# A decode-step gradient kernel on one core: 13 neighbouring rows of the MLP's inner index per partition

## The chip, the core and the metric

The kernel runs on one core of a Trainium2 chip. The metric is the device time of one execution in microseconds (us). A core has a matrix engine (PE, with its weight loads listed apart as PEld), a vector engine (DVE), a scalar engine (ACT), GpSimd (POOL), a sync engine (SP), and 16 DMA engines. DMAs are issued here by SP (queue q1, nearly all loads), POOL (queue q0, the big stores) and ACT (queue q10, the weight gradients' stores). SBUF has 128 partitions.

## The reference, cut to what matters

One transformer layer for a single new position per batch (two batches): layer norm, attention over a cache of 4096 keys and values with 32 heads of 128, then layer norm and an MLP of inner width 1728 with ReLU. The kernel computes the output and, for a given `grad_out`, the gradients of `x`, both caches, and all four weights.

```python
def _A_ref(x, k_cache, v_cache, wq, wo):           # x: 2 x 1 x 640, caches: 2 x 32 x 4096 x 128
    q = (x @ wq) per head
    p = softmax(q . k * 128 ** -0.5); o = p . v
    return o @ wo
def _B_ref(x, w1, w2):                             # w1: 640 x 1728, w2: 1728 x 640
    h = maximum(x @ w1, 0)
    return h @ w2
h = x + _A_ref(_layernorm(x), ...)
h2 = h + _B_ref(_layernorm(h), w1, w2)
# outputs: h2, and the vjp of (x, k_cache, v_cache, wq, wo, w1, w2) at grad_out
```

The caches and their gradients are 67 MB each for keys and for values, read and written once (values are read again for the backward pass, but for the 11 heads kept); they make up nearly all bytes. The MLP's inner index of 1728 is what the change is about: 13 x 128 = 1664 rows and a remainder of 64.

## The kernel before, in words

**Order of the work.** The program's order is written out by hand. A plan of iterations loops over the 64 pairs of batch and head. Phase 1 (`p1_iter`, one iteration per pair) loads K and V (1 MB each), transposes them on PE (L423, evicted by ACT at L428 or DVE at L426), multiplies with q (L436), takes the exponent (L512), forms `pk` on DVE (L464) and `m` and `u` on PE (L457, L486). After batch 0's 32 heads come seven iterations in which phase 1 goes on with batch 1 while batch 0's MLP is worked in between; from then on phase 2 (`p2_iter`) runs beside phase 1, and alone once phase 1 has ended. Phase 2 loads V again (`Wt`) for all but 11 kept heads, and forms the caches' gradients gK and gV on DVE (L818), which POOL stores 1 MB at a time (L856, L875).

**Background work.** Three lists of generators are advanced between the steps of the iterations. A `yield` of a number is the credit that a step takes; `turn()` hands out slots for long DVE products. `middle_gen(b)` is batch b's MLP: it finishes the attention output, normalises (`ln_fwd`), and computes the hidden layer `hf_ps` with w1 as the stationary operand, 14 chunks of up to 128 columns by 5 chunks of the input (L744, 70 matmuls). ReLU gives `acol` (L747). The gradient `ghfc` of the hidden layer (L763) is spread over all partitions as a row, `fbc`: `bcast_cols` makes four chunks at a time on PE (L622) in bank "bc" and ACT evicts them (L625). DVE then takes 15 products of w1 with a third of `fbc` each (L644, "junk" and "gx2p"). The evictions of `fbc` are interleaved: two before the first five products, one before the next five, one before the last. In batch 0 "bc" has two PSUM banks, in batch 1 one.

**w2.** `load_w2` brings w2 in three tiles, of six, six and two chunks. The first time (phase 1, after iterations 8, 13 and 18, for `ga_gen`) chunk c holds rows c*128 to c*128+127, one row of 1,280 bytes per partition and chunk. The second time (`mlp_out`, L698, in phase 2) the tile has whole stretches: partition p holds rows 13p to 13p+12, of which a tile takes six (7,680 bytes). To match, batch 1's middle computes the hidden layer once more in that order, for both batches: `ar_ps`, 65 matmuls whose weights are columns of w1 in steps of 13 (L755), into `arow` (L758).

**Stores of the weights' gradients.** `fin_gen` makes rows of the needed columns (`rows_of`: a copy `wide` at L888, a matmul at L893, an eviction at L895), and `outer_rows` their outer products: a matmul (L922) and an ACT eviction (L928) per 512 columns, several rows per partition gathered in a tile `ot`, and one store (L930, ACT's queue). w2's gradient `out_7` is stored from 96 partitions with 18 rows each, six rows at a time: three stores of 96 x 7,680 bytes.

**Queues.** SP issues all loads in the order of a list; its first two DMAs load A_x and grad_out into `xr` (L210, L211), ahead of wq (L378). SP waits when a tile's buffer is not free (12 big buffers, more in phase 2). ACT and PE execute in the program's order.

Of the kernel before, what the change touches and what calls it, by code (L numbers as in the profile page):

```python
# [7 lines left out]
FP32 = mybir.dt.float32  # L8
BF16 = mybir.dt.bfloat16
ALU = mybir.AluOpType  # L10
# [5 lines left out]
def kernel(  # L16
# [20 lines left out]
    nc = tc.nc  # L37
# [19 lines left out]

    def f_kc(c):
        return 128 if c < NFF else F_rem


    ctx.enter_context(tc.manual_schedule())
# [127 lines left out]
    arow = cols.tile([128, NF, B], BF16)  # L190
    OFc = cols.tile([128, H, B], BF16)
    GQc = cols.tile([128, H, B], BF16)
    qsc = cols.tile([128, H, B], BF16)
# [13 lines left out]
    nc.vector.memset(acol[:], 0.0)  # L207
    nc.vector.memset(ghfc[:], 0.0)

    nc.sync.dma_start(out=xr[0:2 * ND, :], in_=A_x.rearrange("b s (c p) -> (b s c) p", p=128))  # L210
    nc.sync.dma_start(out=xr[2 * ND:4 * ND, :], in_=grad_out.rearrange("b s (c p) -> (b s c) p", p=128))  # L211


    def colsum(src, n):
# [138 lines left out]
    FP = 6  # L353
    NW2 = -(-NF // FP)
    w2_tiles = {}

    def load_w2(k, tag, order="(c p) d -> p c d"):

        c0, c1 = k * FP, min(NF, (k + 1) * FP)
        t = take(tag, [128, FP, D], "w2_t")  # L360
        full = min(c1, NFF)
        if full > c0:
            nc.sync.dma_start(out=t[:, 0:full - c0, :],
                              in_=B_w2[0:NFF * 128, :].rearrange(order, p=128)[:, c0:full, :])
# [247 lines left out]
        nc.vector.tensor_tensor(out=Uc[:, b, :], in0=t[:], in1=rt[:, b, :], op=ALU.mult)  # L612


    def bcast_cols(colsrc, n, kc_of, dst):

        for c0 in range(0, n, 4):
            t = pst([128, 512], FP32, "bc", "bc_ps")
            w = 0
            for c in range(c0, min(n, c0 + 4)):  # L620
                kc = kc_of(c)
                nc.tensor.matmul(t[:, w:w + kc], lhsT=colsrc[0:kc, c:c + 1].to_broadcast([kc, 128]),  # L622
                                 rhs=ident_bf[0:kc, 0:kc], start=True, stop=True)
                w += kc
            nc.scalar.copy(out=dst[:, c0 * 128:c0 * 128 + w], in_=t[:, 0:w])  # L625
            yield

    def spread_cols(t, colsrc, n):
# [26 lines left out]
    def one(src, b):  # L655
        return src[:, :, b]
# [34 lines left out]
    def mlp_out():  # L691

        ml32 = small.tile([128, ND, B], FP32, tag="ml32", bufs=1, name="ml32")
        nc.vector.memset(ml32[:], 0.0)
        for k in range(NW2):
            while free["q"] < 1:
                yield
            t = load_w2(k, "q", "(p c) d -> p c d")  # L698
# [12 lines left out]
        nc.vector.tensor_copy(out=ml_bf[:], in_=ml32[:])  # L711
        y_bf = small.tile([128, B, ND], BF16, tag="y_bf", bufs=1, name="y_bf")
        nc.vector.tensor_tensor(out=y_bf[:].rearrange("p b c -> p c b"), in0=h1c[:], in1=ml_bf[:], op=ALU.add)
        yield from wait(3)
        for b in range(B):
            store_row(y_bf[:, b, :], ND, out_0[b].rearrange("s (c p) -> (s c) p", p=128))
            yield

    def middle_gen(b):
# [21 lines left out]
        for cf in range(NF):  # L741
            kc = f_kc(cf)
            for c in range(ND):
                nc.tensor.matmul(hf_ps[0:kc, cf:cf + 1], lhsT=w1_t[:, c, cf * 128:cf * 128 + kc],  # L744
                                 rhs=x2c[:, c, b:b + 1], start=(c == 0), stop=(c == ND - 1))
            yield 0.25
        nc.vector.tensor_scalar(out=acol[:, 0:NFF, b], in0=hf_ps[:, 0:NFF], scalar1=0.0, scalar2=None, op0=ALU.max)  # L747
        if F_rem:
            nc.vector.tensor_scalar(out=acol[0:F_rem, NFF, b:b + 1], in0=hf_ps[0:F_rem, NFF:NF],
                                    scalar1=0.0, scalar2=None, op0=ALU.max)  # L750
        if b == B - 1:
            ar_ps = pst([128, NFF, B], FP32, "mid", "ar_ps")
            for cf in range(NFF):
                for c in range(ND):
                    nc.tensor.matmul(ar_ps[:, cf, :], lhsT=w1_t[:, c, bass.ds(cf, 128, step=NFF)],  # L755
                                     rhs=x2c[:, c, :], start=(c == 0), stop=(c == ND - 1))
                yield 0.25
            nc.vector.tensor_scalar(out=arow[:, 0:NFF, :], in0=ar_ps[:], scalar1=0.0, scalar2=None, op0=ALU.max)  # L758
            if F_rem:
                nc.vector.tensor_copy(out=arow[:, NFF, :], in_=acol[:, NFF, :])  # L760
# [5 lines left out]
        gx2 = small.tile([128, 1, ND], FP32, tag="gx2", bufs=1, name="gx2")  # L766
        gx2p = small.tile([128, ND, 3], FP32, tag="gx2p", bufs=1, name="gx2p")
        FW = Dff // 3
        spread_f = bcast_cols(one(ghfc, b), NF, f_kc, fbc)
        have = 0  # L770
        for k in range(3):
            while have < min(Dff, (k + 1) * FW):
                next(spread_f)
                have += 512
                yield
            for c in range(ND):
                yield from turn()
                ttr(w1_t[:, c, k * FW:(k + 1) * FW], fbc[:, k * FW:(k + 1) * FW], gx2p[:, c, k:k + 1], FW)
                yield 0.85
# [99 lines left out]

    fw = [0]  # L880

    def rows_of(pool, col, n, name, tag):

        r = pool.tile([128, n * 128], BF16, tag=tag, bufs=2 if tag == "rD" else 1, name=name)
        for c0 in range(0, n, 4):
            cn = min(4, n - c0)
            w = FIN["wide"][(c0 // 4) % 2]
            nc.scalar.copy(out=w[:, 0:cn, :, 0:B], in_=col[:, c0:c0 + cn, None, :].to_broadcast([128, cn, 4, B]))  # L888
            yield
            yield  # L890
            t = pst([128, 512], FP32, "mid", "rw_ps")
            for k in range(cn):
                nc.tensor.matmul(t[:, k * 128:(k + 1) * 128], lhsT=w[:, k, :, :].rearrange("p q x -> p (q x)"),  # L893
                                 rhs=ident_bf[:], start=True, stop=True)
            nc.scalar.copy(out=r[:, c0 * 128:(c0 + cn) * 128], in_=t[:, 0:cn * 128])  # L895
            yield 0.7
        FIN[name] = r

    FIN = {}

    late = [False]

    def outer_rows(L, nrow, R, N, out_ap, cc):


        P = nrow // cc
        grp = max(1, min(cc, 4096 // N))
        out_v = out_ap.rearrange("(p c) n -> p c n", c=cc)
        for c0 in range(0, cc, grp):
            gn = min(grp, cc - c0)  # L910
            while not rested("f", 13):
                yield 0.0
            ot = take("f", [128, grp, N], "ot")
            todo = [(k, n0, min(512, N - n0)) for k in range(gn) for n0 in range(0, N, 512)]
            made = []
            for x in range(len(todo) + 1):
                if x < len(todo):
                    k, n0, nn = todo[x]
                    q = 32 * (fw[0] % 4)
                    o_ps = pst([128, 512], FP32, "o", "o_ps")  # L920
                    fw[0] += 1
                    nc.tensor.matmul(o_ps[0:P, 0:nn], lhsT=L[q:q + B, bass.ds(c0 + k, P, step=cc)],  # L922
                                     rhs=R[q:q + B, n0:n0 + nn], start=True, stop=True)
                    made.append((o_ps, k, n0, nn))
                    yield 0.3
                if x > 0:
                    o_ps, k, n0, nn = made[x - 1]
                    nc.scalar.copy(out=ot[0:P, k, n0:n0 + nn], in_=o_ps[0:P, 0:nn])  # L928
                    yield 0.3
            nc.scalar.dma_start(out=out_v[:, c0:c0 + gn, :], in_=ot[0:P, 0:gn, :])  # L930
            give(ot)

    def fin_gen(fin):
        FIN["wide"] = [fin.tile([128, 4, 4, 32], BF16, tag="wide", bufs=2, name="wide") for _ in range(2)]
# [299 lines left out]
```

## Time and profile before, and how to read it

| | |
|---|---|
| runs | 908.7, 908.89, 909.97 us; median 908.89 us |
| profiled execution | span 905.5 us from the first to the last instruction; it has no time of its own beside this span |
| busy | PE 742.8 us (82%), PEld 620.3, DVE 696.1 (77%), ACT 444.7, POOL 192.4 |
| bytes | 362.87 MB in 56,254 packets, mean 401 GB/s |
| DMA queues | q1 58.1% of the 16 engines' span, q0 35.9%, q10 4.2% |
| TensorE clock granted | 0.780 in the mean: full up to 293 us, mostly half after 470 us |
| w2's loads | four of 960 KB (two in each pass), and the remainders of 160 and 80 KB |
| out_7's stores | three of 720 KB |

The page shows the span in 40 equal slices of 22.6 us, each digit being the busy tenths of an engine. The DMA row is the mean busy share of the 16 DMA engines, and the row below what they moved. The chain of waits follows the last instruction back to what released it. In timelines a row has the start, the time, the engine, the line, the operation, and in brackets how long the engine sat idle and what ended it. Matmuls overlap with the loads of the next weights, so for the cost of a series of small matmuls the time of the series is divided by their number.

### The profile page before, as it was taken

The page shows a single profiled execution, that of the slowest core. Times are in us where ns is not written, and L with a number is a line of the kernel's source. Part 1 is how long each engine was busy: PE and PEld are TensorE (multiplying, and loading weights), DVE is VectorE, ACT ScalarE, POOL GpSimd, SP SyncE. Part 2 cuts the span into 40 slices and gives each one's busy share as a digit, 9 for nine tenths or more (in the row PEclk, how much of TensorE's full clock was granted, in tenths as well). Part 3 has the DMA queues.
Part 4 walks back from the last instruction along what each step waited for, and adds up shares of the span by engine and source line. Part 5 has one row for each costly group of instructions (what it writes and reads, how often), then busy time and mean ns, then how long its engine had stood idle before and what let it go on. Part 6 is the DMA issues. An engine that isn't in the chain of part 4 may idle for free.

```text
span 905.5 us, 24516 instructions
## 1 busy us (share of the span) xinstructions
PE 742.8 (82%) x10205; PEld 620.3 (68%) x10205; DVE 696.1 (77%) x1286; ACT 444.7 (49%) x1096; POOL 192.4 (21%) x330
## 2 busy tenths in 40 slices
PE   3999899899998997987968854877899879859880
PEld 3887788788887887876857744655667656645560
DVE  2666787777888796777869698986898349989982
ACT  1444343344554564554543434644576656637750
POOL 1344433443211110010011111211122111111120
PEclk9999999999999899999885776655555555555655
DMA  8999999999879999999999999999999999999997
GB/s 361 420 409 403 409 398 410 420 417 388 335 306 377 377 406 425 421 424 421 411 398 392 411 423 394 423 398 396 407 401 388 426 420 423 419 423 416 419 421 296
DMA packets 56254, 362.87 MB, mean 401 GB/s; under 512 B 5680, under 2 KB 11696, under 8 KB 15312
## 3 DMA queue, kind: packets, MB, share of 16 engines
q1 hardware_dynamic: 34704, 212.18, 58.1%
q0 software_dynamic: 18432, 134.23, 35.9%
q10 hardware_dynamic: 3008, 14.91, 4.2%
q8 instruction: 80, 1.31, 0.6%
q14 instruction: 30, 0.25, 0.1%
HBM read 212.16 MB, written 149.13 MB: 399 GB/s over the span
## 4 chain that ended last, share of the span: by engine, by line
PE 42%; DMA 25%; DVE 18%; issue 6%; ACT 6%; SPq 1%; POOL 0%; POOLq 0%; ACTq 0%; DVEq 0%
PE t_ps L423 18%; DMA Vt<-in_A_v_cache_dram 13%; PE m_ps L457 9%; DVE gV L818 5%; DMA out_dram<-gV 4%; DVE gK L818 4%; DMA out_dram<-gK 3%; PE s_ps L436 3%; ACT t_sb L428 3%; DMA wqs<-in_A_wq_dram 3%; DVE gxj L644 2%; PE u_ps L486 2%; PE o_ps L922 2%; PE dp_ps L436 2%; DVE pk L464 2%
## 5 line engine op out<-in xcount | busy, mean ns | idle before, releaser
L428 ACT COPY t_sb<-t_ps 128x512 f32<-128x512 f32 x479 | 274.4, 586 | 214.6 <-PE t_ps L423 208.9
L436 PEld LDWEIGHTS <-t_sb 128*128 128x128 bf16 x4096 | 179.0, 102 | 47.0 <-issue 18.8
L423 PE MATMUL t_ps<-ident_f,Wt 128*128 128x128 f32 x848 | 196.5, 379 | 0.2 <-ACT t_sb L428 0.2
L457 PE MATMUL m_ps<-pk,Vt 128*128 128x129 bf16 x2048 | 171.0, 222 | 19.5 <-DMA Vt<-in_A_v_cache_dram 18.2
L464 DVE TENSOR_TENSOR pk<-Kt,ep 128x2048 bf16<-128x2048 bf16 x128 | 156.5, 1223 | 33.9 <-PE m_ps L457 15.8
L818 DVE TENSOR_TENSOR gK<-rb,gsp 128x2048 bf16<-128x2048 bf16 x128 | 152.4, 1225 | 18.4 <-DMA out_dram<-gV 16.4
L818 DVE TENSOR_TENSOR gV<-rb,pp 128x2048 bf16<-128x2048 bf16 x128 | 153.0, 1219 | 15.1 <-DMA out_dram<-gK 12.5
L423 PE MATMUL t_ps<-ident_f,Kt 128*128 128x128 f32 x1024 | 155.1, 284 | 6.6 <-DMA Kt<-in_A_k_cache_dram 6.3
L423 PEld LDWEIGHTS t_ps<-ident_f,Wt 128*128 128x128 f32 x848 | 135.7, 196 | 35.1 <-issue 29.3
L457 PEld LDWEIGHTS <-Vt 128*128 128x128 bf16 x2048 | 124.5, 98 | 51.0 <-issue 29.7
L423 PEld LDWEIGHTS t_ps<-ident_f,Kt 128*128 128x128 f32 x1024 | 112.6, 144 | 10.9 <-PE s_ps L436 4.6
L474 POOL COPY pk<-ep 128x16 bf16<-128x16 bf16 x80 | 83.2, 1042 | 163.6 <-ACT ep L512 87.8
L436 PE MATMUL dp_ps<-gom,t_sb 128*128 128x2 bf16 x2048 | 95.6, 168 | 8.5 <-ACT t_sb L428 7.5
L875 POOL DMA_DIRECT2D out_dram<-gV x64 | 34.2, 534 | 268.0 <-DVE gV L818 207.7
L856 POOL DMA_DIRECT2D out_dram<-gK x64 | 34.0, 532 | 264.9 <-DVE gK L818 207.8
L436 PE MATMUL s_ps<-qm,t_sb 128*128 128x2 bf16 x2048 | 87.4, 164 | 1.5 <-DVE t_sb L426 1.5
L928 ACT CAST ot<-o_ps 128x512 bf16<-128x512 f32 (+4 forms) x160 | 70.4, 490 | 14.8 <-DMA out_dram<-ot 11.2
L571 ACT CAST MT<-m_ps 128x128 bf16<-128x128 f32 x64 | 17.1, 267 | 104.3 <-PE m_ps L457 104.2
L845 ACT ACTIVATE rb<-dp_ps,rt 128x256 bf16<-128x256 f32 x64 | 30.3, 474 | 69.4 <-PE dp_ps L840 68.7
L644 DVE CUSTOM_DVE_ANT_0 junk<-wo_t,hbc 128x640 bf16<-128x640 bf16 x64 | 52.4, 819 | 0.2
L644 DVE CUSTOM_DVE_ANT_0 gxj<-wqs,gqr 128x1024 bf16<-128x1024 bf16 x40 | 48.8, 1221 | 2.4 <-DMA wqs<-in_A_wq_dram 2.2
L831 DVE SCALAR_TENSOR_TENSOR gsp<-dp_ps,negdot,P_bf 128x64 bf16<-128x64 f32 x64 | 18.0, 281 | 42.3 <-PE dp_ps L436 42.0
(198 smaller groups left out, 719.5 us busy)
## 6 DMA issues: line engine op xcount, KB each, us to landing
Kt<-in_A_k_cache_dram SPq DMA_DIRECT2D x64, 1024.0 KB, 16.0
Vt<-in_A_v_cache_dram SPq DMA_DIRECT2D x64, 1024.0 KB, 15.9
out_dram<-gV POOLq DMA_DIRECT2D x64, 1024.0 KB, 14.7
out_dram<-gK POOLq DMA_DIRECT2D x64, 1024.0 KB, 14.4
Wt<-in_A_v_cache_dram SPq DMA_DIRECT2D x53, 1024.0 KB, 11.8
wq_t<-in_A_wq_dram SPq DMA_DIRECT2D x5, 1024.0 KB, 9.2
wo_t<-in_A_wo_dram SPq DMA_DIRECT2D x4, 1280.0 KB, 19.1
wqs<-in_A_wq_dram SPq DMA_DIRECT2D x5, 1024.0 KB, 17.1
```

The costliest lines, as they stand in the source:

```text
L423: nc.tensor.transpose(t_ps[:, j, :], natf[:, 2 * cc:2 * cc + 2, :].rearrange("p c k -> p (c k)"), ident_f[:])
L428: nc.scalar.copy(out=t_sb[:], in_=t_ps[:])
L436: nc.tensor.matmul(dst[:, sc:sc + 2], lhsT=v[:, j, :, par], rhs=vecs[:, par, :], start=(par == 0), stop=(par == 1))
L457: nc.tensor.matmul(r["m"][:, 0:129], lhsT=r["V"][:, sc, :], rhs=r["pk"][sc // HALF][:, sc % HALF, 0:129], start=(sc == 0), stop=(sc == NSC ...
L464: nc.vector.tensor_tensor(out=p["pk"][k][:, :, 0:128].rearrange("p s (a two) -> p s a two", two=2), in0=p["K"][:, sl, :].rearrange("p s (a ...
L474: nc.gpsimd.tensor_copy(out=col, in_=e)
L644: nc.vector.tensor_tensor_reduce(out=junk[0:kc, 0:width], in0=in0, in1=in1, scale=1.0, scalar=0.0, op0=ALU.mult, op1=ALU.add, accum_out=acc)
L818: nc.vector.tensor_tensor(out=pairs_view(dst[:, sl, :]), in0=row.rearrange("p (a two) -> p a two", two=2)[:, None, :, :].to_broadcast([128 ...
L845: nc.scalar.activation(out=rb[:], in_=bank[:, 128:384], func=ACT.Copy, scale=rt[:, b, h:h + 1])
L856: nc.gpsimd.dma_start(out=natural(out_2, bp, hp), in_=gK[:])
L875: nc.gpsimd.dma_start(out=natural(out_3, b, h), in_=gV[:])
L928: nc.scalar.copy(out=ot[0:P, k, n0:n0 + nn], in_=o_ps[0:P, 0:nn])
```

## The change

The inner index of the MLP is laid out in one way everywhere: partition p, chunk c is row 13p + c (the remainder of 64 stays behind).

- `f_sl` selects w1's columns in steps of 13 for L744, in both batches; `by_f` evicts the rows `fbc` and `ghfr` so that the chunks interleave (in steps of 13 elements, 26 bytes, in what ACT writes), in five pieces each where there were four.
- `arow` and its 65 matmuls go; the second use of w2 takes `acol`.
- w2's first loads take whole stretches of rows too: 7,680 bytes per partition in place of six pieces of 1,280.
- `out_7` is written by a function of its own, `w2_rows`, from 128 partitions with 13 rows each, in groups of 5, 4 and 4 rows, and one store of the 64 remaining rows. `outer_tile` is the loop that it shares with `outer_rows`.
- All of `fbc` is made before the first product with it.
- The two loads of `xr` are issued by ACT, not SP.

```diff
+    def f_sl(c):
+        return bass.ds(c, 128, step=NFF) if c < NFF else slice(NFF * 128, Dff)
+
+    def by_f(dst, t, c0, cn):
+        full = min(cn, NFF - c0)
+        if full > 0:
+            nc.scalar.copy(out=dst[:, 0:NFF * 128].rearrange("q (p c) -> q c p", c=NFF)[:, c0:c0 + full, :],
+                           in_=t[:, 0:full * 128].rearrange("q (c p) -> q c p", p=128))
+        if full < cn:
+            nc.scalar.copy(out=dst[:, NFF * 128:Dff], in_=t[:, full * 128:full * 128 + F_rem])
...
-    nc.sync.dma_start(out=xr[0:2 * ND, :], in_=A_x.rearrange("b s (c p) -> (b s c) p", p=128))
-    nc.sync.dma_start(out=xr[2 * ND:4 * ND, :], in_=grad_out.rearrange("b s (c p) -> (b s c) p", p=128))
+    nc.scalar.dma_start(out=xr[0:2 * ND, :], in_=A_x.rearrange("b s (c p) -> (b s c) p", p=128))
+    nc.scalar.dma_start(out=xr[2 * ND:4 * ND, :], in_=grad_out.rearrange("b s (c p) -> (b s c) p", p=128))
...
-    def load_w2(k, tag, order="(c p) d -> p c d"):
+    def load_w2(k, tag):
...
-                              in_=B_w2[0:NFF * 128, :].rearrange(order, p=128)[:, c0:full, :])
+                              in_=B_w2[0:NFF * 128, :].rearrange("(p c) d -> p c d", p=128)[:, c0:full, :])
...
-                                     rhs=arow[0:kc, cf, :], start=(cf == k * FP), stop=(cf == c1 - 1))
+                                     rhs=acol[0:kc, cf, :], start=(cf == k * FP), stop=(cf == c1 - 1))
...
-                nc.tensor.matmul(hf_ps[0:kc, cf:cf + 1], lhsT=w1_t[:, c, cf * 128:cf * 128 + kc],
+                nc.tensor.matmul(hf_ps[0:kc, cf:cf + 1], lhsT=w1_t[:, c, f_sl(cf)],
                                  rhs=x2c[:, c, b:b + 1], start=(c == 0), stop=(c == ND - 1))
...
-        if b == B - 1:
-            ar_ps = pst([128, NFF, B], FP32, "mid", "ar_ps")
-            for cf in range(NFF):
-                for c in range(ND):
-                    nc.tensor.matmul(ar_ps[:, cf, :], lhsT=w1_t[:, c, bass.ds(cf, 128, step=NFF)],
-                                     rhs=x2c[:, c, :], start=(c == 0), stop=(c == ND - 1))
-                yield 0.25
-            nc.vector.tensor_scalar(out=arow[:, 0:NFF, :], in0=ar_ps[:], scalar1=0.0, scalar2=None, op0=ALU.max)
...
-        spread_f = bcast_cols(one(ghfc, b), NF, f_kc, fbc)
-        have = 0
+        yield from bcast_cols(one(ghfc, b), NF, f_kc, fbc, True)
         for k in range(3):
-            while have < min(Dff, (k + 1) * FW):
-                next(spread_f)
-                have += 512
-                yield
...
+    def w2_rows(L, R):
+        out_v = out_7[0:NFF * 128, :].rearrange("(p c) n -> p c n", c=NFF)
+        c0 = 0
+        for gn in (5, 4, 4):
...
+            todo = [(lambda q, c=c: L[q:q + B, c * 128:c * 128 + f_kc(c)], f_kc(c), k, n0, min(512, D - n0))
+                    for c, k in cs for n0 in range(0, D, 512)]
+            stores = [(out_v[:, c0:c0 + gn, :], ot[:, 0:gn, :])]
+            if last:
+                stores.append((out_7[NFF * 128:Dff, :], ot[0:F_rem, gn, :]))
+            yield from outer_tile(todo, R, ot, stores)
...
-        yield from outer_rows(FIN["ar"], Dff, FIN["gr"], D, out_7, Dff // 96)
-        yield from rows_of(fin, ghfc, NF, "ghfr", "rX")
+        yield from w2_rows(FIN["ar"], FIN["gr"])
+        yield from rows_of(fin, ghfc, NF, "ghfr", "rX", True)
```

More of the change, by code (lines that the diff above doesn't have):

```diff
@@ L189 @@
     ghfc = cols.tile([128, NF, B], BF16)
-    arow = cols.tile([128, NF, B], BF16)
     OFc = cols.tile([128, H, B], BF16)
@@ L612, in u_out, with bcast_cols @@
         nc.vector.tensor_tensor(out=Uc[:, b, :], in0=t[:], in1=rt[:, b, :], op=ALU.mult)
-    def bcast_cols(colsrc, n, kc_of, dst):
+    def bcast_cols(colsrc, n, kc_of, dst, f_order=False):
         for c0 in range(0, n, 4):
@@ L624, in bcast_cols @@
                 w += kc
-            nc.scalar.copy(out=dst[:, c0 * 128:c0 * 128 + w], in_=t[:, 0:w])
+            if f_order:
+                by_f(dst, t, c0, min(4, n - c0))
+            else:
+                nc.scalar.copy(out=dst[:, c0 * 128:c0 * 128 + w], in_=t[:, 0:w])
             yield
@@ L697, in mlp_out @@
                 yield
-            t = load_w2(k, "q", "(p c) d -> p c d")
+            t = load_w2(k, "q")
             yield from wait(12)
@@ L750, in middle_gen @@
                                     scalar1=0.0, scalar2=None, op0=ALU.max)
-        if b == B - 1:
-            ar_ps = pst([128, NFF, B], FP32, "mid", "ar_ps")
-            for cf in range(NFF):
-                for c in range(ND):
-                    nc.tensor.matmul(ar_ps[:, cf, :], lhsT=w1_t[:, c, bass.ds(cf, 128, step=NFF)],
-                                     rhs=x2c[:, c, :], start=(c == 0), stop=(c == ND - 1))
-                yield 0.25
-            nc.vector.tensor_scalar(out=arow[:, 0:NFF, :], in0=ar_ps[:], scalar1=0.0, scalar2=None, op0=ALU.max)
-            if F_rem:
-                nc.vector.tensor_copy(out=arow[:, NFF, :], in_=acol[:, NFF, :])
         mask = small.tile([128, NF], FP32, tag="mask", bufs=1, name="mask")
@@ L880, with rows_of @@
     fw = [0]
-    def rows_of(pool, col, n, name, tag):
+    def rows_of(pool, col, n, name, tag, f_order=False):
         r = pool.tile([128, n * 128], BF16, tag=tag, bufs=2 if tag == "rD" else 1, name=name)
@@ L894, in rows_of @@
                                  rhs=ident_bf[:], start=True, stop=True)
-            nc.scalar.copy(out=r[:, c0 * 128:(c0 + cn) * 128], in_=t[:, 0:cn * 128])
+            if f_order:
+                by_f(r, t, c0, cn)
+            else:
+                nc.scalar.copy(out=r[:, c0 * 128:(c0 + cn) * 128], in_=t[:, 0:cn * 128])
             yield 0.7
@@ L901, with outer_tile @@
     late = [False]
+    def outer_tile(todo, R, ot, stores):
+        made = []
+        for x in range(len(todo) + 1):
+            if x < len(todo):
+                row, P, k, n0, nn = todo[x]
+                q = 32 * (fw[0] % 4)
+                o_ps = pst([128, 512], FP32, "o", "o_ps")
+                fw[0] += 1
+                nc.tensor.matmul(o_ps[0:P, 0:nn], lhsT=row(q), rhs=R[q:q + B, n0:n0 + nn], start=True, stop=True)
+                made.append((o_ps, P, k, n0, nn))
+                yield 0.3
+            if x > 0:
+                o_ps, P, k, n0, nn = made[x - 1]
+                nc.scalar.copy(out=ot[0:P, k, n0:n0 + nn], in_=o_ps[0:P, 0:nn])
+                yield 0.3
+        for out_ap, src in stores:
+            nc.scalar.dma_start(out=out_ap, in_=src)
+        give(ot)
     def outer_rows(L, nrow, R, N, out_ap, cc):
@@ L913, in outer_rows @@
             ot = take("f", [128, grp, N], "ot")
[L914 to L931, printed above, removed]
+            todo = [(lambda q, k=k: L[q:q + B, bass.ds(c0 + k, P, step=cc)], P, k, n0, min(512, N - n0))
+                    for k in range(gn) for n0 in range(0, N, 512)]
+            yield from outer_tile(todo, R, ot, [(out_v[:, c0:c0 + gn, :], ot[0:P, 0:gn, :])])
+    def w2_rows(L, R):
+        out_v = out_7[0:NFF * 128, :].rearrange("(p c) n -> p c n", c=NFF)
+        c0 = 0
+        for gn in (5, 4, 4):
+            while not rested("f", 13):
+                yield 0.0
+            ot = take("f", [128, 6, D], "ot")
+            last = c0 + gn == NFF
+            cs = [(c0 + k, k) for k in range(gn + int(last))]
+            todo = [(lambda q, c=c: L[q:q + B, c * 128:c * 128 + f_kc(c)], f_kc(c), k, n0, min(512, D - n0))
[4 more added lines that the diff above has]
+            yield from outer_tile(todo, R, ot, stores)
+            c0 += gn
     def fin_gen(fin):
```

## The prediction

> **What bounds the kernel now.** I read the page's busy slices first, then the DMA view, then the chain of waits, then windows and timelines. The slices:
>
> ```profile
> PEclk9999999999999899999885776655555555555655
> DMA  8999999999879999999999999999999999999997
> GB/s 361 420 409 403 409 398 410 420 417 388 335 306 377 377 406 425 421 424 421 411 398 392 411 423 394 423 398 396 407 401 388 426 420 423 419 423 416 419 421 296
> ```
>
> The 16 DMA engines are full almost everywhere; a kernel in that state ends when its bytes are moved, so its time is the DMA engines' work plus their idle time. The idle time lies at the start, in slices 10 to 14 (about 204 to 317 us) and at the end. Slices that are full but below 420 GB/s lose something else: packets that cost more than they must. The windows put numbers on both (columns after the engines' busy times: granted clock, DMA share, GB/s):
>
> ```profile
> 140.00:150.00 10.00, 8.72 (x151) 7.35 (x150) 8.07 (x17) 3.97 (x12) 4.18 (x5) 1.00 1.01 419
> 55.80:58.60 2.80, 2.80 (x45) 2.69 (x43) 1.01 (x3) 2.08 (x7) 0.67 (x3) 1.00 1.05 375
> 226.00:249.00 23.00, 21.75 (x375) 19.05 (x375) 20.03 (x52) 12.74 (x35) 5.98 (x10) 1.00 0.88 337
> 500.00:550.00 50.00, 30.15 (x414) 26.54 (x414) 40.51 (x69) 19.84 (x37) 7.83 (x18) 0.70 1.01 421
> 582.00:656.00 74.00, 56.61 (x518) 46.37 (x517) 59.55 (x102) 37.42 (x83) 13.09 (x25) 0.52 1.01 401
> 700.00:760.00 60.00, 47.58 (x440) 36.89 (x440) 32.34 (x36) 36.86 (x77) 7.06 (x16) 0.56 1.01 423
> ```
>
> 226 to 249 us is batch 0's MLP stage: PE and DVE busy for 21.75 and 20.03 of 23 us, DMA idle for an eighth. There compute is the bound, and the chain of waits runs through compute engines alone from 204.9 to 282.1 us. From 582 to 656 us, when out_7 is stored, DMA is full at only 401 GB/s, and the chain names stores: 18.62 us for a gK and 21.59 us for a gV.
>
> **The change, part by part.** Durations are of the one profiled execution, span 905.5 us; the runs' median, 908.89 us, is 3.4 us above it, which I take as fixed.
>
> (1) *Start.* The two loads of xr leave SP's queue:
>
> ```profile
> 0.74 0.41 SPq L210 DMA_DIRECT2D xr<-in_A_x_dram  x1
> 1.21 0.29 SPq L211 DMA_DIRECT2D xr<-in_grad_out_dram  x1
> 1.54 2.62 SPq L378 DMA_DIRECT2D wq_t<-in_A_wq_dram  x5
> ```
>
> SP's first big load goes out at 0.74 instead of 1.54, and all loads behind it move up: -0.8 us while DMA is the bound, down to 0 if ACT's loads only queue among wq's packets. ACT issues them ahead of its table load (1.28 us), which then ends near 2.7; ACT's first copy is at 21.36, so that is covered. The layer norm waits for xr; it ends at 8.8, while the last wq tile lands at 17.7 with 5 us of q matmuls to do before it, so xr may be about 3.7 us late at no cost. Taken: -0.8.
>
> (2) *w2's two early loads* (960 KB each, from 40 and 72 us) consist of 1,280-byte packets now, of 7,680-byte ones afterwards. 55.8 to 58.6 us holds such packets: 1.05 x 2.80 us for 1.05 MB is 2.8 us per MB; 140 to 150 us, all 8 KB packets, is 1.01 x 10 / 4.19 MB = 2.4. The difference, 0.4, times 1.97 MB: -0.8 us (0 if compute is the bound there; the chain waits for V loads up to 166 us, so I take all).
>
> (3) *Batch 0's hidden layer* (L744) reads its weights from w1 in steps of 13 columns. Such loads exist only at L755, at half clock, where L744 stands beside it:
>
> ```profile
> 495.96 0.94 PE L744 MATMUL hf_ps<-x2c,w_t 128*128 128x1 bf16 x20
> 503.07 1.36 PE L755 MATMUL ar_ps<-x2c,w_t 128*128 128x2 bf16 x20
> ```
>
> That is 47 ns a pair in neighbouring columns and 68 in steps; at full clock L744 takes 26 (1.83 us of the chain for batch 0's 70). Scaled with the clock, 68 becomes 37 and 70 pairs lose 0.8 us; kept at 68 they lose 2.9. A gain is excluded: the same columns are read in more places. On the chain. Taken: the middle, +1.9.
>
> [...]
>
> (4) *Batch 0's fbc.* The order of instructions in the built program: all five evictions of fbc now precede the first product of L644, since strided writes reach every third of it. Now:
>
> ```profile
> 229.88 1.08 ACT L625 CAST fbc<-bc_ps 128x512 bf16<-128x512 f32 x2
> 230.95 0.59 ACT L428 COPY t_sb<-t_ps 128x512 f32<-128x512 f32 x1
> 230.99 0.76 DVE L644 CUSTOM_DVE_ANT_0 junk<-w_t,fbc 128x576 bf16<-128x576 bf16 x1 [0.31 <-ACT fbc L625]
> ```
>
> DVE starts at 230.99, on the heels of two evictions. Afterwards: the third group of four matmuls waits for the first of the two banks (free at 230.5), so PE does it until 231.1 and ACT evicts it until 231.75; behind it PE does m, s and t_ps (1.0 us, to 232.1), ACT copies t_sb (0.59, to 232.7), then the last two pieces (0.27 and about 0.2): 233.2. DVE loses 2.3 us in a stage that it nearly fills, less 0.2 for the two groups that no longer interrupt PE later. Taken: +2.1. Low end 1.65 (ACT's three copies and t_sb alone), high end 3.3: whether ACT pays for a 26-byte step in what it writes no row shows for 512 elements (16 elements at L476 with a 260-byte step take 263 ns, 32 at L888 take 222); at the weight loads' ratio 68/47 the five would take 1.0 us more. I hold to no penalty.
>
> (5) *Batch 1's stage* loses the 65 strided matmuls of arow, 4.5 us of PE and a 5.35 us wait of DVE, and pays 70 x 21 ns = 1.5 us at L744; its five fbc evictions go through one bank. The windows say what that is worth: DMA is full at 421 GB/s from 500 to 550 us and behind by stores already issued. Taken: 0, between -2 (the 30 us from 470 ran at 395 GB/s instead of 421, 1.9 us) and +1.5. The chain names ar_ps in this stretch, but freeing it means only that stores join a full queue sooner.
>
> (6) *out_7's store.* Three stores of 96 partitions x 7,680 bytes become stores of 128 partitions x 6,400, 5,120 and 5,120 bytes and 80 KB more. The DMA view of three stretches, q10 being ACT's queue and q0 the gK and gV stores (columns: packets, MB, share of 16 engines):
>
> ```profile
> q0 software_dynamic: 226, 1.68, 45.5%
> q10 hardware_dynamic: 111, 0.74, 26.5%
> ```
>
> from 587 to 597 us, and from 700 to 760 us, when out_5 is stored from 128 partitions in the same 7,680-byte pieces:
>
> ```profile
> q0 software_dynamic: 1654, 12.04, 47.9%
> q10 hardware_dynamic: 432, 2.62, 10.4%
> ```
>
> q10 pays 2.65 us for 0.74 MB, 3.6 us per MB, against 6.24 / 2.62 = 2.4; q0 pays 2.71 against 2.39. The second and third store (612 to 626, 640 to 650 us) show q10 at 2.46 and 1.83 us for 0.74 MB, q0 at 2.68 and 2.56 per MB. Excess over 2.38: 1.7 us on q10, 0.5 + 0.8 + 0.4 = 1.7 on q0. If 128 partitions behave like out_5: -3.4 us. High end 0 (the cause is another), low end -3.8 (all 74 us at 423 GB/s instead of 401). Taken: -3.4, by out_5's row. Eight matmuls and eight evictions fewer (28 instead of 36) save about 3.4 us of ACT in a stage that DMA bounds: nothing.
>
> [...]
>
> (7) *The rest.* Fifth evictions and strided ones in ghfr (about 0.2 us), the fin and gx work one pass of phase 2 earlier: no idle DMA to win, 0. The end stays a drain: the last store is issued at 889.39 and DMA is full to 898.
>
> Sum: -0.8 - 0.8 + 1.9 + 2.1 + 0 - 3.4 = **-1.0 us**, 907.9.
>
> **The rivals.**
> *A, faster.* (3) and (4) at their low ends, 2.45, and (5) at -2: -0.8 - 0.8 + 2.45 - 2 - 3.4 = -4.6, **904.3**. For it: the chain runs through ar_ps and PE's loads may follow the clock. Against it: DMA full from 500 us on.
> *B, slower: transfers hidden anyway.* Chain pieces between 166 and 282 us are compute, so what DMA saves before may not arrive, and the store queue may be fed no sooner: only (3) + (4) = +4.0 are left, **912.9**. It decides as soon as compute, not loads, sets the pace before 166 us. Against it: V loads of 11.6 to 16.9 us on the chain there.
> *C, slower: the stores don't get cheaper*, since out_7's place in memory and not the 96 partitions costs. Without -3.4: **911.3**. For it: the third store was nearly clean with the same partitions. Against it: out_5's and out_6's stores, all clean.
> That the change doesn't move what it says is excluded: the built program has 128x3840 in one piece for w2.
>
> **How the numbers follow.** Forecast 0.40, A 0.29, C 0.17, B 0.14. About 0.2% (1.8 us) is what a measurement of this kernel can tell from no change: 907.1 to 910.7. The forecast's own range, 906 to 910, lies there for some 0.28 of its 0.40, 0.09 below and 0.03 above; C leaves 0.04 inside. Faster 0.38, same 0.32, slower 0.30. All high ends together give +7.7, all low ones -5.0; with the cases' weights 903.5 to 913.0 leaves out about 2 in 10.
>
> **What would show it.** (1) wq's first issue at 0.74. (2) no window under 400 GB/s at 55 us. (3) L744 at full clock at 35 to 70 ns a pair. (4) the first product of L644 about 2 us later behind fbc, and DMA share below 0.88 around it. (6) q10 near 2.4 us per MB during out_7. It is wrong if DMA idles elsewhere: after 450 us, say, because stores and loads meet in another order.

## The result and the profile after

The changed kernel takes 919.56 us (median of 6 runs, 918.49 to 922.1) against 909.09 for the kernel before (6 runs, 905.64 to 912.1): ratio 1.0111, 95% interval 1.0082 to 1.014, about 10 us slower. Beside the later experiments it took 921.45 (5 runs) against 910.04 (ratio 1.012, 1.0092 to 1.0147). Here and below, differences in us are of medians; the ratios are those on record, which are not quotients of the medians and imply up to some 2 us more or less. The forecast of 907.9 and its range up to 913.0 are both missed. The profiled execution took 919.25, its span is 916.8.

Three rows of the page after, each over 40 slices of 22.9 us (PE's granted clock, the DMA engines' busy share, and what they moved):

```profile
PEclk9999899899799899897995576655555555575565
DMA  9999999999488999999999999999999999999997
GB/s 378 420 414 414 411 400 410 419 409 359 163 317 336 382 390 424 425 423 423 421 408 400 390 349 424 422 420 417 403 423 394 417 357 425 424 426 424 424 424 323
```

The hole is slice 11, 229 to 252 us, where the middle part of batch 0 is worked: 163 GB/s. The windows answer puts the rest beside it (columns: stretch, its length, busy us and instructions of PE, PEld, DVE, ACT and POOL, granted clock, DMA share, GB/s):

```profile
226.00:249.00 23.00, 19.86 (x244) 17.38 (x243) 8.69 (x23) 13.35 (x21) 2.39 (x5) 0.70 0.41 155
520.00:540.00 20.00, 14.56 (x153) 12.89 (x152) 14.25 (x23) 11.82 (x17) 2.08 (x5) 0.53 0.83 328
582.00:656.00 74.00, 52.14 (x498) 40.87 (x497) 61.35 (x109) 39.76 (x79) 12.96 (x27) 0.52 1.01 419
```

From 226 to 249 us DMA is busy 0.41 of the time and DVE 8.69 us of 23 (before: 0.88 and 20.03). A second hole lies at 520 to 540, where batch 1's middle part is worked: 0.83. The same stretch of the kernel before:

```profile
520.00:540.00 20.00, 11.84 (x170) 9.98 (x169) 19.31 (x32) 9.06 (x17) 3.92 (x9) 0.79 1.01 423
```

The prediction had named DMA idling after 450 us as a sign of being wrong. During out_7's stores, 582 to 656, the change does good: 419 GB/s for 401.

What happens in the first hole, from the timeline of the same execution (start, time, engine, line):

```profile
225.15 1.92 PE L759 MATMUL hf_ps<-x2c,w_t 128*128 128x1 bf16 x30
227.40 1.30 PE L759 MATMUL hf_ps<-x2c,w_t 128*128 128x1 bf16 x20
229.21 1.41 PE L759 MATMUL hf_ps<-x2c,w_t 128*128 128x1 bf16 x20
...
235.02 6.86 ACT L69 CAST fbc<-bc_ps 128x512 bf16<-128x512 f32 x3
...
242.21 0.71 ACT L69 CAST fbc<-bc_ps 128x128 bf16<-128x128 f32 x1
...
242.42 0.54 ACT L72 CAST fbc<-bc_ps 128x64 bf16<-128x64 f32 x1
...
242.95 0.76 DVE L659 CUSTOM_DVE_ANT_0 junk<-w_t,fbc 128x576 bf16<-128x576 bf16 x1 [8.13 <-ACT fbc L69]
```

L759 is the line that was L744, L69 and L72 are `by_f`, L659 was L644. Three evictions of 128x512 take 6.86 us, 2.3 each, where they took 0.59; DVE waits 8.13 us for them. The first product comes 17.8 us after the first hidden layer matmul; before it was 6.6 (to 230.99, from this row of the kernel before):

```profile
224.39 0.89 PE L744 MATMUL hf_ps<-x2c,w_t 128*128 128x1 bf16 x30
```

The chain of waits of the changed kernel, cut to this stretch, now runs through ACT:

```profile
234.44 0.58 ACT t_sb L440
235.02 3.97 ACT fbc L69 x2
239.15 2.73 ACT fbc L69
241.88 0.42 ACT t_sb L440
242.31 0.62 ACT fbc L69
242.95 0.76 DVE junk L659
```

Up to 214 us the n-th K load is issued within some 2.5 us of its time before, except the 16th, which is 6.6 earlier; the 40th comes at 246.2 for 234.2, 12 us later. The lag varies from there on, and the last store is issued 11.7 us late (901.12 for 889.39).

### The profile page after: what moved, and what is told of

It reads as the page before. It is cut to its first block, busy times and chain, and to the rows that moved or that the text cites. A ratio compares the mean times of both kernels' runs of the same rounds, so it can differ in the third digit from the quotient of the medians.

```text
span 916.8 us, 24369 instructions
## 1 busy us (share of the span) xinstructions
PE 744.8 (81%) x10132; PEld 623.5 (68%) x10132; DVE 695.6 (76%) x1284; ACT 459.1 (50%) x1091; POOL 189.7 (21%) x330
## 3 DMA queue, kind: packets, MB, share of 16 engines
q8 instruction: 79, 1.29, 0.5%
## 4 chain that ended last, share of the span: by engine, by line
PE 44%; DVE 20%; DMA 20%; ACT 6%; issue 6%; SPq 0%; POOL 0%; POOLq 0%; ACTq 0%; DVEq 0%
PE t_ps L435 18%; DMA Vt<-in_A_v_cache_dram 10%; PE m_ps L469 10%; DVE gV L818 5%; DMA out_dram<-gV 5%; DMA out_dram<-gK 4%; DVE gK L818 4%; PE s_ps L448 3%; DVE junk L659 3%; DVE gxj L659 3%; PE u_ps L498 3%; DVE pk L476 3%; PE dp_ps L448 2%; ACT t_sb L440 2%; PE o_ps L915 2%
## 5 line engine op out<-in xcount | busy, mean ns | idle before, releaser
L435 PE MATMUL t_ps<-ident_f,Wt 128*128 128x128 f32 x848 | 194.0, 376 | 0.2 <-ACT t_sb L440 0.2
L469 PE MATMUL m_ps<-pk,Vt 128*128 128x129 bf16 x2048 | 174.8, 225 | 16.5 <-DMA Vt<-in_A_v_cache_dram 15.1
L476 DVE TENSOR_TENSOR pk<-Kt,ep 128x2048 bf16<-128x2048 bf16 x128 | 156.5, 1223 | 30.3 <-ACT ep L524 14.0
L435 PE MATMUL t_ps<-ident_f,Kt 128*128 128x128 f32 x1024 | 160.1, 291 | 6.4 <-DMA Kt<-in_A_k_cache_dram 6.4
L469 PEld LDWEIGHTS <-Vt 128*128 128x128 bf16 x2048 | 127.6, 100 | 48.0 <-issue 29.3
L435 PEld LDWEIGHTS t_ps<-ident_f,Kt 128*128 128x128 f32 x1024 | 116.6, 148 | 10.3 <-issue 6.4
L448 PE MATMUL dp_ps<-gom,t_sb 128*128 128x2 bf16 x2048 | 95.5, 168 | 12.8 <-ACT t_sb L440 12.2
L583 ACT CAST MT<-m_ps 128x128 bf16<-128x128 f32 x64 | 17.1, 267 | 108.8 <-PE m_ps L469 108.7
L920 ACT CAST ot<-o_ps 128x512 bf16<-128x512 f32 (+3 forms) x152 | 67.6, 494 | 4.0 <-DMA out_dram<-ot 1.7
L659 DVE CUSTOM_DVE_ANT_0 junk<-wo_t,hbc 128x640 bf16<-128x640 bf16 x64 | 52.4, 818 | 0.2
L659 DVE CUSTOM_DVE_ANT_0 gxj<-wqs,gqr 128x1024 bf16<-128x1024 bf16 x40 | 48.8, 1219 | 0.2
```

The source lines that it names most:

```text
L435: nc.tensor.transpose(t_ps[:, j, :], natf[:, 2 * cc:2 * cc + 2, :].rearrange("p c k -> p (c k)"), ident_f[:])
L448: nc.tensor.matmul(dst[:, sc:sc + 2], lhsT=v[:, j, :, par], rhs=vecs[:, par, :], start=(par == 0), stop=(par == 1))
L469: nc.tensor.matmul(r["m"][:, 0:129], lhsT=r["V"][:, sc, :], rhs=r["pk"][sc // HALF][:, sc % HALF, 0:129], start=(sc == 0), stop=(sc == NSC ...
L476: nc.vector.tensor_tensor(out=p["pk"][k][:, :, 0:128].rearrange("p s (a two) -> p s a two", two=2), in0=p["K"][:, sl, :].rearrange("p s (a ...
L659: nc.vector.tensor_tensor_reduce(out=junk[0:kc, 0:width], in0=in0, in1=in1, scale=1.0, scalar=0.0, op0=ALU.mult, op1=ALU.add, accum_out=acc)
```

## The experiments

"Order" means that all pieces of fbc are made before the first product, "steps" that weights are read 13 columns apart. The first four experiments ran on one chip, beside a kernel before of 909.91 us (30 runs); the next four on another with 910.04 (23 runs), the last two on a third with 908.36 (13 runs).

**Contiguous writes of fbc.** Edit to the changed kernel:

```diff
-            nc.scalar.copy(out=dst[:, 0:NFF * 128].rearrange("q (p c) -> q c p", c=NFF)[:, c0:c0 + full, :],
-                           in_=t[:, 0:full * 128].rearrange("q (c p) -> q c p", p=128))
+            nc.scalar.copy(out=dst[:, c0 * 128:(c0 + full) * 128], in_=t[:, 0:full * 128])
...
-        for k in range(3):
+        for k in (2, 1, 0):
```

> The changed kernel, but the evictions of fbc and ghfr write neighbouring elements in place of every 13th (so the inner index of these rows is out of order and the gradients that follow from them are not the reference's); same five pieces, all ahead of the first product, and the thirds are taken last first, so that the first product still waits for the last pieces. Only the step of what ACT writes is gone. Theory 1 (ACT pays for the step: 2.37 us against 0.59 for 512 elements, DVE waits 8.1 us for it in batch 0 and 8.7 us in batch 1): about 910 us, 9 to 10 us less than the change's 919.6; DVE's wait for fbc in batch 0 under 3 us. Theory 2 (the weights in steps of 13 hold PE and with it everything): 917 to 919, little moves. Theory 3 (it is the order, all pieces ahead of the first product): 916 to 919, the order is still there.

Measured: 909.05 us, ratio to before 0.9996 (0.9971 to 1.002). Undoing this one thing takes back the whole loss against the kernel before, as theory 1 has it. The first product comes 12.8 us behind the first matmul.

**Neighbouring columns as weights.** Edit to the changed kernel:

```diff
-        return bass.ds(c, 128, step=NFF) if c < NFF else slice(NFF * 128, Dff)
+        return slice(c * 128, c * 128 + 128) if c < NFF else slice(NFF * 128, Dff)
```

> The changed kernel, but the hidden layer reads neighbouring columns of w1 as weights (so its inner index is in another order than w2's rows, and what follows is not the reference's); the strided evictions stay. Theory 1: about 917 us, 2.8 us less than the change (70 pairs in batch 0 at 26 ns in place of 66). Theory 2: near 909, the change's loss is gone. Theory 3: as theory 1.

Measured: 910.91 us, ratio 1.0019 (0.9995 to 1.0043); the first product after 13.4 us. So this gains 8.6 too (against 919.56, from another chip), where theory 1 expected 2.8. Both terms are large, and the two single gains (10.5 and 8.6) add up to more than what was lost; the next experiments take that up.

**The order alone**, on the kernel before:

```diff
-        spread_f = bcast_cols(one(ghfc, b), NF, f_kc, fbc)
-        have = 0
-        for k in range(3):
-            while have < min(Dff, (k + 1) * FW):
-                next(spread_f)
-                have += 512
-                yield
+        yield from bcast_cols(one(ghfc, b), NF, f_kc, fbc)
+        for k in (2, 1, 0):
```

> The kernel before, but all four evictions of fbc come ahead of the first product, and the thirds are taken last first, so that the first product waits for the last piece: step (4) of the prediction alone, without any step in what is written. Theory 1: 909 to 911.5, 0 to 2.1 us over the kernel before. Theory 3: 915 to 919.

Measured: 912.83 us, ratio 1.003 (1.0009 to 1.0051), +2.9; the first product after 8.35 us, 1.75 later than before. That is above the 909 to 911.5 expected, but the interval, 0.8 to 4.6 us over the kernel before, takes in the +2.1 that the prediction has for the order.

**Start and store**, on the kernel before: `xr` loaded by ACT, and out_7 stored from 128 partitions, with the rows picked in steps from the row of acol.

```diff
-    nc.sync.dma_start(out=xr[0:2 * ND, :], in_=A_x.rearrange("b s (c p) -> (b s c) p", p=128))
+    nc.scalar.dma_start(out=xr[0:2 * ND, :], in_=A_x.rearrange("b s (c p) -> (b s c) p", p=128))
... (grad_out likewise; w2_rows and outer_tile added)
-        yield from outer_rows(FIN["ar"], Dff, FIN["gr"], D, out_7, Dff // 96)
+        yield from w2_rows(FIN["ar"], FIN["gr"])
```

> The kernel before with the two parts of the change that touch no layout: the loads of xr issued by ACT, and out_7 stored from 128 partitions, 13 rows each (its rows picked in steps of 13 from the row tile as it was). If DMA work saved reaches the end, as the prediction had it: -0.8 and -3.4, about 905 us. If the transfers are hidden anyway (rival B): 908 to 910, the same as before.

Measured: 902.65 us, ratio 0.9929 (0.9901 to 0.9957), 7.3 us faster than before, more than the 4.2 expected.

**The changed kernel again, beside the next three.**

> The changed kernel once more, beside the three others of this comparison. The two single undoings together gain more than the whole loss: undoing ACT's strided writes 10.5 us, undoing the weights in steps 8.6, 19.1 in sum, while the loss to be explained is 919.6 - 902.7 (start and store alone) = 16.9, of which 2.9 is the order. Theory X (the two hold each other up in batch 0's stage, so either undoing frees a part of both): 918 to 921 again. Theory Y (the changed kernel's time belonged to other conditions than the experiments'): 914 to 916, so that the two terms add up to about 14.

Measured: 921.45 us. The loss is as large on this chip, and theory Y falls: the gains of the two single experiments don't simply add.

**Both undone**: the edits of the first two experiments together.

> The changed kernel with both undone: contiguous writes of fbc and ghfr, and neighbouring columns as weights for the hidden layer. (The columns of the hidden layer then stand in another order than the rows of w2 that they meet, so the MLP's results are those of another product; the work is the same.) What is left of the change is the start, w2's long rows, out_7's store and the order (all five pieces of fbc before the first product). From the kernel before: -7.3 (start and store, measured together) + 2.9 (order, measured alone) - 0.8 (w2's early loads) = 904 to 906. If it is over 908, something else in the changed kernel costs time that none of the single experiments has touched. If it is near 900.5 (919.6 - 10.5 - 8.6), the two terms simply add and the order's 2.9 does not apply here.

Measured: 904.71 us, ratio 0.996 (0.9935 to 0.9986), in the range named. Nothing else in the change costs time that would show beside this interval of some 2 us to either side. The first product comes after 8.4 us, as with the order alone.

**The store alone**: the second half of the edit of "start and store".

> The kernel before with only out_7's store changed to 128 partitions. Theory 'start and store add as the prediction has them' (-0.8 and -3.4, scaled to the measured -7.3): 903.5 to 904.5, the store bringing -5.5 to -6.5. Theory 'the store is worth what its queue time says': -3.4, 906.5. Theory 'the start brings most': 908 to 909.

Measured: 902.68 us, ratio 0.9929 (0.9901 to 0.9958). The store brings the whole gain that was measured, more than any of the three theories had. The earlier start brings 0.0 in the medians; with intervals of some 2.6 us to either side, the 0.8 predicted for it can be neither seen nor excluded by these times. This kernel is the fastest of the study, together with "start and store", and faster than both kernels of the case.

**The same writes in runs of four**: the changed kernel, with the two loops of the eviction exchanged. The places written are the same.

```diff
-            nc.scalar.copy(out=dst[:, 0:NFF * 128].rearrange("q (p c) -> q c p", c=NFF)[:, c0:c0 + full, :],
-                           in_=t[:, 0:full * 128].rearrange("q (c p) -> q c p", p=128))
+            nc.scalar.copy(out=dst[:, 0:NFF * 128].rearrange("q (p c) -> q p c", c=NFF)[:, :, c0:c0 + full],
+                           in_=t[:, 0:full * 128].rearrange("q (c p) -> q p c", p=128))
```

> The changed kernel with the five evictions of fbc (and ghfr's) writing the same elements to the same places in another order: four neighbouring elements at a time (8 bytes), then a step of 26 bytes, where the changed kernel writes 128 elements at a step of 26 bytes, four times over. ACT reads PSUM with the step instead (512 bytes). Theory 1 (ACT pays for each written element that stands apart from the one before it): 128 places instead of 512, the eviction falls from 2.37 us to between 0.6 and 0.9, and the kernel to 909 to 912, as with contiguous writes. Rival (any access in steps costs the same, read or written, or the cost is for the two-dimensional pattern): 2.3 us or more as before, 918 to 921.

Measured: 909.3 us, ratio 0.9988 (0.9967 to 1.0008), 12 us less than the changed kernel on the same chip. Its timeline in batch 0:

```profile
234.47 2.07 ACT L69 CAST fbc<-bc_ps 128x512 bf16<-128x512 f32 x3
...
237.95 0.81 DVE L659 CUSTOM_DVE_ANT_0 junk<-w_t,fbc 128x576 bf16<-128x576 bf16 x1 [3.68 <-ACT fbc L69]
```

The three evictions take 2.07 us, 0.69 each, where the changed kernel has 2.29; theory 1 holds. Against this kernel the changed one loses time in two places. Up to 214 us their loads go out together (within 1 us); from the 40th K load on, at 241 us, the changed kernel is 5.0 late, and stays near that (4.3 to 8.8) until 515; by 530 it is 10 late (19th second load of V: 528.9 against 539.0; in the second profile of the changed kernel 540.0), and 8 to 11 to the end. The second step is batch 1's stage. The 520 to 540 us row of this kernel stands beside the changed kernel's 0.83 above:

```profile
520.00:540.00 20.00, 16.89 (x216) 14.28 (x214) 19.79 (x33) 12.53 (x23) 3.93 (x9) 0.80 1.01 406
```

**The weights in steps alone**, on the kernel before:

```diff
-                nc.tensor.matmul(hf_ps[0:kc, cf:cf + 1], lhsT=w1_t[:, c, cf * 128:cf * 128 + kc],
+                nc.tensor.matmul(hf_ps[0:kc, cf:cf + 1], lhsT=w1_t[:, c, bass.ds(cf, 128, step=NFF) if cf < NFF else slice(NFF * 128, Dff)],
```

> The kernel before with one thing from the change: the hidden layer's weights in steps of 13 columns (so acol comes in another order than fbc and w2's rows expect, and the MLP's results are those of another product; the work is the same). By the rows: 70 pairs at 64 ns instead of 26 in batch 0 is +2.7 us; in every trace with such weights a stretch of half clock falls just behind these matmuls and adds 1.8 us until the first product. Theory P (the stretch comes with these weights): the first product 11 us behind the first matmul, and the kernel at +4 to +5, 914 to 915. Theory Q (the stretch falls there by chance): 9.3 us behind, and +2 to +3, 912 to 913. Rival R (DMA hides it, as in batch 1): within 1 us of the kernel before.

Measured: 913.78 us (908.67 to 920.74) against 908.36, ratio 1.007 (1.0043 to 1.0098), +5.4; the first product after 10.4 us. The time is near theory P, and R falls; the first product lies between P's 11 and Q's 9.3. The profiled execution was this kernel's fastest run, and its stretch of half clock was short (229.3 to 232.7 us), so it decides less than the time does.

**The disputed costs by themselves.**

```diff
...
+    for s in (1, 2, 4, 8, 13, 16, 32):
+        nc.scalar.copy(out=wo_f[:, 0:512 * s].rearrange("p (n s) -> p n s", s=s)[:, :, 0], in_=pr_src[:])
+    nc.scalar.copy(out=wo_f[:, 0:512], in_=pr_src[:].rearrange("p (a b) -> p b a", a=4))
+    nc.scalar.copy(out=wo_f[:, 0:128 * 13].rearrange("p (n c) -> p n c", c=13)[:, :, 0:4],
+                   in_=pr_src[:].rearrange("p (c n) -> p n c", c=4))
...
+    for s in (1, 4, 8, 13):
+        nc.vector.tensor_copy(out=w1_f[:, 0:512 * s].rearrange("p (n s) -> p n s", s=s)[:, :, 0], in_=pr_src[:])
...
+    for s in (1, 2, 4, 8, 13, 16):
+        for k in range(30):
+            nc.tensor.matmul(pr_out[:, k:k + 1], lhsT=w1_f[:, bass.ds(0, 128, step=s)], rhs=w1_f[:, 0:1],
+                             start=True, stop=True)
```

> The disputed costs by themselves, on the kernel before with instructions added in its first 30 us whose results nothing reads: ACT copies of 128x512 from PSUM to SBUF (bfloat16) with 1, 2, 4, 8, 13, 16 and 32 elements from one written element to the next; one with contiguous writes and PSUM read in steps of 128; one with writes in runs of four elements (8 bytes) at a step of 13; VectorE copies with steps of 1, 4, 8 and 13; then 30 matmuls each with weight columns 1, 2, 4, 8, 13 and 16 apart. Theory 1 (ACT pays per written element once the step leaves some width): 0.59 us at step 1, 2.37 at 13 and the same at 16 and 32, runs of four near 0.80, strided reads near 0.59; between 2 and 8 the width shows. Rival: the cost grows with the step, so 32 is far above 13. VectorE: unknown, 0.6 us if it pays nothing, 2.4 if it is a matter of SBUF's write side. Weights: 26 ns a pair at step 1 and 64 at step 13; if any step costs, 2 is at 64 already. The kernel's own time rises by what these add at the start, 20 to 40 us; that is no result.

One run, 919.55 us; its profile has the single operations. ACT in windows cut at its copies' starts (columns: stretch, length, ACT's busy us and instructions, clock, DMA share, GB/s); in order steps 1, 2, 4, 8, 13, 16, 32, then the read in steps, then runs of four:

```profile
9.46:10.08 0.62, 0.58 (x1) 1.00 1.03 436
10.08:10.84 0.76, 0.73 (x1) 1.00 1.03 431
10.84:12.16 1.32, 1.29 (x1) 1.00 0.97 410
12.16:14.61 2.45, 2.42 (x1) 1.00 1.01 428
14.61:17.01 2.40, 2.37 (x1) 1.00 1.02 430
17.01:19.34 2.33, 2.29 (x1) 1.00 1.01 422
19.34:21.74 2.40, 2.38 (x1) 1.00 1.01 420
21.74:22.36 0.62, 0.58 (x1) 1.00 1.02 423
22.36:23.17 0.81, 0.78 (x1) 1.00 1.05 435
```

The cost rises to 2.42 us at a step of 8 elements (16 bytes) and then stays (2.29 to 2.38). An estimate from these rows: what is paid is not the step but each stretch of 16 bytes that is touched anew, some 4.6 ns (2.37 / 512). It is rough: for steps of 2 and 4 elements, 128 and 256 such stretches, it gives 0.59 and 1.18 us, and 0.73 and 1.29 were measured. The read in steps costs nothing here (0.58 us, as at step 1). VectorE, same windows, steps 1, 4, 8 and 13:

```profile
23.18:23.89 0.71, 0.69 (x1) 1.00 0.91 381
23.89:25.22 1.33, 1.29 (x1) 1.00 1.05 437
25.22:27.67 2.45, 2.42 (x1) 1.00 1.00 415
27.67:30.10 2.43, 2.37 (x1) 1.00 1.01 421
```

From a step of 4 on these are the same prices, to 0.01 us (at step 1 it is 0.69 for ACT's 0.58). So the price is not ACT's alone; where it arises these rows don't show. And 30 weight loads each with steps 1, 2, 4, 8, 13, 16 (columns: stretch, length, PE, PEld, clock, DMA share, GB/s):

```profile
31.29:32.10 0.81, 0.80 (x30) 0.81 (x31) 1.00 1.02 425
32.10:32.90 0.80, 0.80 (x36) 0.80 (x34) 1.00 0.93 389
32.90:33.90 1.00, 1.00 (x36) 1.00 (x34) 1.00 0.01 0
33.90:35.70 1.80, 1.80 (x35) 1.80 (x34) 1.00 0.03 9
35.70:37.50 1.80, 1.80 (x33) 1.80 (x33) 1.00 0.00 0
37.50:39.38 1.88, 1.88 (x33) 1.88 (x32) 1.00 0.00 0
```

The first three stretches last 0.8, 0.8 and 1.0 us, the last three 1.8: 27, 27, 33, 60, 60 and 62 ns a pair from the matmuls' starts (the counts in brackets take in neighbours at the edges). Nothing is paid at 2 columns, 6 ns at 4, and from 8 columns, 16 bytes, on the time stays, as with the writes. The expectation that 2 would cost as much as 13 falls.

## Why the prediction was wrong, point by point

The time from the first hidden layer matmul to the first product in batch 0, in the profiles, shows the main terms (us; "half clock" is whether a stretch of it, granted clock 0.50, falls in between):

| kernel | order | steps | ACT's step | half clock | time |
|---|---|---|---|---|---|
| before, store alone | | | | no | 6.6, 6.6 |
| order alone; both undone | yes | | | no | 8.35, 8.4 |
| start and store | | | | yes | 8.8 |
| steps alone | | yes | | yes | 10.4 |
| contiguous writes | yes | yes | | yes | 12.8 |
| neighbouring columns | yes | | yes | during ACT's evictions | 13.4 |
| runs of four | yes | yes | small | yes | 13.4 |
| after, twice | yes | yes | yes | yes | 17.8, 17.8 |

*Step (4) is the one that failed.* It took the place in the order and the bank's turn right (+2.1 predicted; 1.75 in this table, 2.9 in the time of the order alone) and then held that ACT pays nothing for a 26-byte step in what it writes. It pays 1.8 us per 128x512 (2.37 for 0.59). In batch 0 that is +5.0 us on the chain (17.8 - 12.8); the high end allowed for 1.0, from the ratio of the weight loads, 68 to 47. That ratio stems from half clock; at full clock the same loads show 64 to 30 (1.92 and 0.89 us for 30); the rows at L476 and L888, with 16 and 32 elements (263 and 222 ns), are too short to show a price per element. No row excluded a higher price, so the high end should have stayed open; it was closed by a ratio from another engine.

*Step (5)* failed with it: it took 0, with a high end of +1.5, because DMA was full in batch 1's stage. It was, before; the same evictions there, through a single bank, hold DVE 8.7 us and PE 7.5 us, so POOL gets no stores (none is issued from 517.2 to 529.7 us) and DMA runs at 0.83 (0.87 in the second profile) for 20 us:

```profile
525.61 0.76 DVE L659 CUSTOM_DVE_ANT_0 junk<-w_t,fbc 128x576 bf16<-128x576 bf16 x1 [8.69 <-ACT fbc L69]
```

The loss of a further 5 us is seen in the loads. With contiguous writes or runs of four the share is 1.01: "DMA is the bound" held only as long as DVE kept feeding it. ACT's step alone does less here. With neighbouring columns the same evictions hold DVE 5.5 us, and the row is

```profile
520.00:540.00 20.00, 17.53 (x199) 15.69 (x199) 19.79 (x32) 10.66 (x20) 3.92 (x9) 0.59 0.98 385
```

So this second hole comes with the two together; by what path was not tested. *Step (7)* was right to take 0 for `ghfr`, though its three large evictions pay the same price (2.4 us each for 0.58): DMA stays at 1.01 behind them (630 to 652 us).

*Step (3)* came out near its upper end: 64 ns a pair at full clock too (1.92 us for 30), as in the flat reading, not scaled: 2.6 us for the 70 (5.5 us from the first matmul to ReLU, before 3.0); the middle, +1.9, was too little. A further 1.8 us lies between ReLU and the first eviction (4.4 for 2.5), where PE does transposes at half clock (eight in 1.97 us, granted clock 0.50). The time bears it out: +4.4 from "both undone" to "contiguous writes" (904.71 to 909.05, on two chips), +5.4 alone (3.9 to 8.9). Whether these weights bring on the half clock was not settled: in all five profiles with steps it begins 3 to 5 us after the first such matmul (228.2 in the changed kernel); but "start and store" has it at 229.7 without steps, 3.3 us after its first matmul of the hidden layer, and its first product comes 2.2 us later in the table than without one. Earlier stretches don't settle it: six of these profiles have one between 108 and 120 us and one between 160 and 180 (granted clock 0.66 to 0.83 in 110 to 120 us, 0.67 to 0.84 in 160 to 170), and one of the six, "store alone", has none in this stage; "steps alone" has 1.00 in both windows and the stretch here.

*Step (6)* was right that the store gets cheaper, and too small: -3.4 predicted, -7.3 measured (95%: -9.0 to -3.8). ACT's queue q10 now pays what out_5's store pays. From the DMA view of 628 to 640 us in the changed kernel:

```profile
q0 software_dynamic: 448, 3.27, 65.9%
...
q10 hardware_dynamic: 138, 0.64, 13.0%
```

13.0% of 12 us for 0.64 MB is 2.4 us per MB, where the three stores before paid 3.6, 3.3 and 2.5; q0's stores also pay 2.42. In the pair of profiles, store alone against before, the DMA engines' time falls by 4.6 us (98.9% of 900.7 against 98.9% of 905.5), the span by 4.8. The prediction's 3.4 counted three windows only. What the medians show beyond 4.8 lies within their interval. Rival C is refuted.

*Step (1)*: the loads did move up by 0.8 us, `xr` came 3.8 us later and cost nothing (the first transposition starts at 18.20 for 20.21), but no gain at the end is seen: 902.65 with it, 902.68 without. The profiles show where it goes. At the 20th K load "start and store" leads the kernel before by 0.8 us (108.16 for 108.95), and the changed kernel, with w2's long rows too, by 1.6 (107.34). At the 21st the changed kernel is 0.7 behind (117.20 for 116.49): between them lies a stretch of half clock, 108.7 to 115.5 us, that the profile before doesn't have. "Both undone", which has no such stretch before 139 us, still leads by 1.6 us at its hidden layer (222.77 for 224.39). So the lead is there and compute eats it, which is rival B's point; in how many runs, the profiles can't tell. *Step (2)*: the early w2 loads run at 424 GB/s for 375, and the second 0.8 us of that lead is what was predicted; alone it was not tried. "Both undone" less "store alone" is +2.0 for it and the order together, where the order alone is +2.9; that agrees with -0.8 and shows nothing by itself.

The sum, on the second chip: before 910.04, store -7.4, order and w2's loads +2.0, steps and ACT's step together +16.7, after 921.45 (with rounding). Of the 16.7, "runs of four" leaves 4.6, nearly all of it for steps, and 12 is ACT's step in single elements, of which the loads show 5 in each of the two stages. With neighbouring columns, ACT's step costs only 6.2 in the medians (904.71 to 910.91). The loads there lose 5 us in batch 0's stage and some 7 in batch 1's, but of the 7 most comes back by 740 us. The spans of these two profiles are 10.4 apart (911.1 and 900.7), but the one execution lies 2.5 us above its median and the other 2.0 below. The time in which the DMA engines idle (the span less a sixteenth of all packets' times) says more: 10.5 us in "both undone" as in the kernel before, 17.4 and 17.5 with steps ("contiguous writes", "runs of four"), 18.0 with ACT's step and neighbouring columns, 27.3 and 26.8 in the changed kernel. So the two cost about 7.0 and 7.5 us of idle DMA one by one and 16.5 together, close to the 16.7 of the times. Part of the excess is the second hole: from 500 to 550 us DMA is busy 1.00 to 1.01 with either one and 0.94 to 0.95 with both. What stays open is why that hole needs both, and the 1 to 3 us by which the medians of the single ones (4.4, 4.6 and 6.2) fall short of their idle time; each has an interval of some 2 us to either side.

## What to carry to other kernels

Before a layout is given a step, count for every engine that writes it, and for weight loads from it, how many stretches of 16 bytes are touched: here 512 in place of 64 made a copy four times as long on ACT (2.37 us for 0.58) and 3.4 times on DVE (2.37 for 0.69), and columns 8 or more apart made a weight load with its matmul 2.2 times as long (60 ns for 27). The loop order in one access pattern is free to choose: put the few neighbouring elements innermost and the step on the PSUM side (0.69 us for 2.29 here). And "DMA hides it" is worth checking for who feeds the DMA queue: a stage at 423 GB/s fell to 328 when the engine that makes the stores had to wait. A change that is bundled from one good part and several bad ones is best taken apart: the store alone is 0.7% faster than before.

## What the runs showed of the hardware that was not expected

The price of a written element in a 16-byte stretch of its own is the same for ScalarE and VectorE (2.37 us for 512 at a step of 13 on both). Runs of four elements at a 26-byte step cost 0.78 us: 128 runs, of which three in eight straddle two stretches, are 176 stretches, and with the 4.6 ns estimated above 176 of them are 0.81 us. Reading PSUM in steps of 512 bytes cost ACT nothing (0.58 us). Weight loads with a step of 16 bytes or more took 60 to 65 ns a pair with their matmul at full clock, and 63 to 70 at half clock (L759 in the changed kernel, 3.15 us for 50 and 1.41 for 20).
